# Two batches' kv in one call: k and v of batch 5 loaded with batch 4 in a fused linear-attention and MLP kernel

## The chip, the cores and the metric

One NeuronCore of one Trainium2 chip runs the kernel. The metric is the device time of one execution in microseconds. Three runs of the kernel before took 288.9, 288.96 and 289.06 us, so the median is 288.96 us.

## The reference

There are eight batches, eight heads, 576 positions and a head dimension of 64. The first half is linear attention with a norm for each head, the second a two-layer MLP with a layer norm and a residual:

```python
kv = np.einsum('bhsd,bhse->bhde', k, v)
out = np.einsum('bhsd,bhde->bhse', q, kv)
rms = np.sqrt(np.mean(out * out, axis=-1, keepdims=True) + 1e-06)
x = (out / rms * g_norm)          # heads side by side: [8, 576, 512]
xn = (x - mu) / np.sqrt(var + 1e-06) * g_ln
result = x + np.maximum(xn @ w_ch1, 0.0) @ w_ch2    # 512 -> 2048 -> 512
```

So batch b's kv needs all of k and v of that batch, and every row of its output needs that kv.

## The kernel before

**Tiles.** Each batch has 576 positions: four tiles of 128 positions and a remainder of 64. The remainders of two batches are put together into one remainder tile of 128 (`rem_tile`, L364; tile 3 joins batches 2 and 3), and the four remainder tiles make a ninth block called "rem", which the MLP takes last.

**A batch's way to the MLP.** `load` (L92) brings one tensor of a batch into one of two buffers, `k_in`, `v_in` or `q_in` with index b % 2, in two DMAs issued from POOL that also cast f32 to bf16: 320 KB and 256 KB as stored. `kv_of` (L240) makes the kv of one or more batches with 40 matmuls of 64 columns each into one PSUM tile (L247), and copies it to `kv_pack[b % 4]` on ACT (L252, L253). `turn_q_dma` (L202) copies q on DVE into another order (L204) and has SP issue a DMA transpose (L206) that gives `qt`. A tile's work is planned by `plan_tile` (L374) in four steps: the matmuls of q with kv (`o`, L274) with the squares and their sums; the scaling to x and its normed copy `xc`; the variance; and a transpose of `xc` into `xT_blk`, which for the later batches is a DMA transpose issued from SP (L355).

**The MLP.** `mm1` (L406) multiplies the four tiles' `xT_blk` with the first weight (L416) and ACT applies the relu (L419); `mm2` (L455) multiplies with the second weight (L432), DVE adds the residual in `finish` (L437), and the result is stored by DMA from SP (L452, L453).

**The order of the work.** A hand-written agenda sets it. `at(slot, fn)` (L474) files a function under a slot, and `tick` (L477), which mm1 and mm2 call once for every four full-width matmuls, emits what is due before the next matmuls. Each batch takes 32 slots: mm1 of batch b from slot 32b on, and mm2 from 32b + 16 on. All engines execute in the order of emission, and each waits for semaphores of the others. So a function filed under slot 85 puts its TensorE work in the middle of mm2 of batch 2, and its DMAs and copies behind whatever was emitted before on their own engines.

**The gate ahead of a load.** `load_batches` (L96) first copies one element of something to `gate` on POOL (L98), for example the last element of a batch's turned q. POOL can't issue the loads behind it until that has been written. Loads of one call go out in the order of the list.

The part that the change touches is the list of loads (L641 to L647), the list of kv calls with their remainder tiles (L650 to L653), and the list of q turns with their batches' tiles (L658 to L663).

Of the kernel before, what the change touches and what calls it, by code (L numbers as in the profile page):

```python
# [14 lines left out]
def kernel(  # L15
# [76 lines left out]
    def load(dst, t, b, h0=0, h1=H):  # L92
        nc.gpsimd.dma_start(dst[:64, h0:h1], lo(t, b, h0, h1))
        nc.gpsimd.dma_start(dst[64:, h0:h1, :J], up(t, b, h0, h1))

    def load_batches(what, *after):  # L96
        for element in after:
            nc.gpsimd.tensor_copy(gate, element)  # L98
        tensors = {"k": (k_in, k), "v": (v_in, v), "q": (q_in, q)}
        for name, b in what:  # L100
            dst, src = tensors[name]
            load(dst[b % NB], src, b)
# [99 lines left out]
    def turn_q_dma(b):  # L202
        q_p = kv_in.tile([128, JJ, H, D], bf16, tag="qp", bufs=2)
        nc.vector.tensor_copy(q_p.rearrange("p j h d -> p h j d"), q_in[b % NB])  # L204
        q_t = qt_pool.tile([128, JJ, HP, 128], bf16, tag="qt", name="qt")
        nc.sync.dma_start_transpose(  # L206
            q_t.rearrange("p j hp t -> p (j hp) t"), q_p.rearrange("p j h d -> p (j h d)"))
        qts[b] = q_t
# [31 lines left out]
    def kv_of(*bs):  # L240
        kv_ps = ps_m.tile([128, len(bs), HP, D], f32, tag="misc", name="kv_ps")
        for i, b in enumerate(bs):
            for hp in range(HP):
                for j in range(JJ):
                    for hh in range(2):
                        h = 2 * hp + hh
                        nc.tensor.matmul(  # L247
                            kv_ps[hh * D:hh * D + D, i, hp, :], lhsT=k_in[b % NB][:, h, j, :],
                            rhs=v_in[b % NB][:, h, j, :], start=(j == 0), stop=(j == JJ - 1))
        for i, b in enumerate(bs):  # L250
            kvp = held[b] = kv_pack[b % 4]
            nc.scalar.copy(kvp[:D, :, :D], kv_ps[:D, i])  # L252
            nc.scalar.copy(kvp[D:, :, D:], kv_ps[D:, i])  # L253
# [104 lines left out]
    def main_tile(b, j, pool=None, tag="ops"):  # L358
        q_t, kvp = qts[b], held[b]
        if b not in blks:  # L360
            blks[b] = new_block("main", 3)
        return Tile([(slice(0, 128), lambda hp: q_t[:, j, hp, :], kvp)], blks[b], j, pool, tag)

    def rem_tile(b):  # L364
        mms = []
        for half, bb in enumerate((b - 1, b)):
            qt, kp = qts.pop(bb), held.pop(bb)
            mms.append((slice(half * 64, (half + 1) * 64),
                        lambda hp, qt=qt: qt[:, J, hp, :64], kp))
        if "rem" not in blks:  # L370
            blks["rem"] = new_block("rem", 1)
        return Tile(mms, blks["rem"], b // 2)

    def plan_tile(s, make, turn_at, on_pe, x_at=None):  # L374
        box = []

        def first():
            t = make()
            box.append(t)
            t.o()  # L380
            t.sq()
            t.red()

        def second():
            t = box[0]
            t.y()
            t.x()
            t.xc()

        def third():  # L390
            box[0].var()

        def fourth():
            box[0].turn(on_pe)

        at(s, first)
        at(x_at or s + 2, second)
        at((x_at or s + 2) + 4, third)
        at(turn_at, fourth)
# [22 lines left out]
    def rstd_of(b):  # L422
        rstd = work.tile([128, 4], f32, tag="rstd", bufs=3, name="rstd")
        nc.scalar.activation(rstd, blks[b][1][:, 2, :], func=AF.Sqrt, scale=1.0 / Dm, bias=eps_sb)  # L424
        nc.vector.reciprocal(rstd, rstd)  # L425
        rstds[b] = rstd
# [47 lines left out]
    def at(slot, fn):  # L474
        agenda.setdefault(int(slot), []).append((slot, fn))
# [162 lines left out]
    def turned_q(b):  # L638
        return qts[b][:1, J, HP - 1, 127:]

    at(47, lambda: load_batches((("k", 3), ("v", 3), ("q", 3)), turned_q(2)))  # L641
    at(68, lambda: load_batches((("k", 4), ("v", 4), ("q", 4)),
                                turned_q(3), blks[2][2][:1, nK - 1, 511:]))
    at(100, lambda: load_batches((("k", 5), ("v", 5), ("q", 5)), turned_q(4)))
    at(132, lambda: load_batches((("q", 6), ("k", 6), ("v", 6), ("k", 7), ("v", 7)),
                                 turned_q(5)))
    at(164, lambda: load_batches((("q", 7),), turned_q(6)))  # L647


    at(115, lambda: kv_of(5))  # L650
    for s, bs, rem, x_at, tn in ((56, (3,), 1, 64, 69), (85, (4,), 3, 88, 94),
                                 (152, (6, 7), 5, 154, 160)):
        at(s, lambda bs=bs: kv_of(*bs))  # L653
        plan_tile(s + .1, lambda rem=rem: rem_tile(rem), tn, False, x_at)
    plan_tile(210, lambda: rem_tile(7), 216, False)


    for b, at_q, at_o, step in ((3, 56.05, 67, 4.3), (4, 86, 97, 4.75),  # L658
                                *((b, 32 * b - 43.3, 32 * b - 32, 5) for b in range(5, B))):
        at(at_q, lambda b=b: turn_q_dma(b))  # L660
        for j in range(J):
            o = at_o + step * j
            plan_tile(o, lambda b=b, j=j: main_tile(b, j), o + 6, False)  # L663
        at(32 * b + 14, lambda b=b: rstd_of(b))
# [59 lines left out]
```

## Time and profile before

| what | value |
|---|---|
| median of three runs | 288.96 us |
| the profiled execution's own time | 288.75 us |
| its span, first to last instruction | 286.7 us |
| TensorE matmul busy | 277.8 us (97%) |
| VectorE, ScalarE, GpSimd busy | 150.0, 152.9, 43.1 us |
| granted TensorE clock | 1.000 |
| bytes read from HBM, written | 36.71 MB, 9.44 MB |
| one load of 320 KB, issue to landing (median) | 8.7 to 10.3 us |
| one DMA transpose of a tile (median) | 3.2 us |
| one DMA transpose of a batch's q (median) | 5.1 us |

The span is what the profile's times refer to; 2.05 us of the profiled execution's own time lie outside it. Times in a timeline are from the start of the span. A row names the start, the duration, the engine, the line, the operation, what it writes and reads, and how many instructions are merged in it; in brackets stands how long the engine had been idle before, and what ended that. A few matmul records are missing from the trace, so a row that should have 20 can show 19. PE is the matmul part of TensorE, PEld its weight loads. SP issues most stores and all the DMA transposes of this kernel, POOL issues the loads; their DMA rows show the issue, and the landing is shown apart in the DMA view.

In the trace, mm2 of batch 2 begins near 95.7 us, mm1 of batch 3 at 110.62, mm2 of batch 3 at 125.33 and mm1 of batch 4 at 140.23.

### The profile page before, as it was taken

To read this page: it belongs to the slowest core of one execution; us is meant where nothing else is said; L and a number is where in the kernel's file an instruction comes from. 1 tells how busy PE (TensorE), PEld (TensorE's weight loads), DVE (VectorE), ACT (ScalarE), POOL (GpSimd) and SP (SyncE) were. 2 spreads that over 40 slices of the span, in tenths; PEclk is the share of its full clock that TensorE was granted. 3 is DMA by queue.
4 is the path that set the end of the run, shared out by engine and by line. 5 is a ranking of instruction groups with operands and counts; after the bars stand their busy time and mean duration, and the time that the engine had idled before them with its cause. 6 is when DMAs were issued, how large, how long until landed. Compare 5 with 4: busy or idle time off the path is not lost.

```text
span 286.7 us, 5727 instructions
## 1 busy us (share of the span) xinstructions
PE 277.8 (97%) x2269; PEld 158.0 (55%) x2295; DVE 150.0 (52%) x331; ACT 152.9 (53%) x333; POOL 43.1 (15%) x73
## 2 busy tenths in 40 slices
PE   7889999999999999999999999999999999999995
PEld 3579755995579654454444544444444444444444
DVE  5774119937997883774376475763679200220022
ACT  3477844995468643971387338911893066016500
POOL 8522510041036005000710020000000000000000
PEclk9999999999999999999999999999999999999999
DMA  7999999969997979986999995047203410230033
GB/s 215 198 209 202 201 191 197 214 111 188 144 180 124 185 141 172 214 101 127 159 215 190 120 160 135 18 82 158 56 18 72 95 37 0 48 81 19 0 73 76
DMA packets 67419, 36.76 MB, mean 128 GB/s; under 512 B 35517, under 2 KB 62525, under 8 KB 67393
## 3 DMA queue, kind: packets, MB, share of 16 engines
q0 software_dynamic: 28720, 18.29, 44.2%
q1 hardware_dynamic: 38160, 17.39, 30.4%
q10 hardware_dynamic: 512, 0.72, 0.8%
q8 instruction: 18, 0.29, 0.5%
q14 instruction: 9, 0.07, 0.1%
HBM read 36.71 MB, written 9.44 MB: 161 GB/s over the span
## 4 chain that ended last, share of the span: by engine, by line
PE 91%; DMA 2%; DVE 2%; ACT 2%; issue 1%; DVEq 0%; POOLq 0%
PE p L432 43%; PE p L416 42%; PE o_ps L274 3%; DMA v_in<-in_v_dram 2%; PE kv_ps L247 2%; ACT m L419 1%; DVE x_blk L292 0%; DVE xc L552 0%; ACT xT_blk L353 0%; PE tp L351 0%; ACT rms L311 0%; PE odd L226 0%; DVE ss L518 0%; PE tp L559 0%; DVE ss L301 0%
## 5 line engine op out<-in xcount | busy, mean ns | idle before, releaser
L416 PE MATMUL p<-xT_blk,w_sb 128*128 128x128 bf16 (+2 forms) x1015 | 131.2, 285 | 0.9
L432 PE MATMUL p<-w_sb,m 128*128 128x512 bf16 (+2 forms) x592 | 126.2, 368 | 1.2 <-issue 0.5
L419 ACT ACTIVATE m<-p 128x512 bf16<-128x512 f32 x144 | 85.2, 596 | 46.7 <-PE p L416 44.3
L416 PEld LDWEIGHTS <-w_sb 128*128 128x128 bf16 x1024 | 78.6, 98 | 44.5 <-issue 1.1
L432 PEld LDWEIGHTS <-m 128*128 128x128 bf16 x608 | 57.3, 98 | 62.9
L437 DVE SCALAR_TENSOR_TENSOR o_sb<-p,rstd,x_blk 128x512 f32<-128x512 f32 (+2 forms) x38 | 27.2, 721 | 47.7 <-PE p L432 42.1
L280 ACT ACTIVATE sq<-o_ps 128x512 f32<-128x512 f32 x35 | 20.9, 596 | 26.7 <-PE o_ps L274 26.5
L343 ACT ACTIVATE dev<-x_blk,st_blk 128x512 f32<-128x512 f32 x36 | 25.7, 714 | 13.1 <-DVE st_blk L329 13.1
L301 DVE TENSOR_REDUCE ss<-sq 128x8 f32<-128x512 f32 x35 | 23.7, 678 | 17.0 <-ACT sq L280 17.0
L335 DVE SCALAR_TENSOR_TENSOR xc<-x_blk,st_blk,g_ln_sb 128x512 bf16<-128x512 f32 x34 | 25.6, 752 | 1.2
L306 DVE TENSOR_TENSOR y<-o_ps,inv 128x512 f32<-128x512 f32 x33 | 22.8, 692 | 3.1
L325 DVE SCALAR_TENSOR_TENSOR x_blk<-y,g_norm_sb 128x512 f32<-128x512 f32 x33 | 22.8, 692 | 1.1
L318 DVE RECIPROCAL inv<-rms 128x8 f32<-128x8 f32 x36 | 7.3, 202 | 23.3 <-ACT rms L311 23.3
L425 DVE RECIPROCAL rstd<-rstd 128x4 f32<-128x4 f32 x9 | 1.6, 175 | 29.9 <-ACT rstd L424 29.8
L311 ACT ACTIVATE rms<-ss,eps_sb 128x8 f32<-128x8 f32 x36 | 10.6, 295 | 11.5 <-DVE ss L301 11.3
L274 PEld LDWEIGHTS <-qt 128*128 128x128 bf16 (+1 forms) x156 | 10.3, 100 | 6.0 <-issue 0.4
L274 PE MATMUL o_ps<-kv_pack,qt 128*128 128x128 bf16 (+1 forms) x156 | 13.6, 220 | 0.0
L98 POOL COPY gate<-qt 1x1 bf16<-1x1 bf16 x5 | 0.9, 177 | 82.4 <-DMA qt<-q_p 82.4
L199 PE MATMUL p<-fill_sb 128*128 128x512 bf16 x26 | 7.8, 452 | 1.3 <-DVE eps_sb L138 1.2
L252 ACT CAST kv_pack<-kv_ps 64x256 bf16<-64x256 f32 x7 | 2.6, 366 | 10.7 <-PE kv_ps L247 10.7
L343 ACT ACTIVATION_READ_ACCUMULATOR dev<-x_blk,st_blk 128x1 f32 x36 | 6.8, 190 | 0.0
L247 PEld LDWEIGHTS <-k_in 128*64 128x64 bf16 x280 | 4.9, 112 | 2.4 <-issue 2.3
(82 smaller groups left out, 112.6 us busy)
## 6 DMA issues: line engine op xcount, KB each, us to landing
out_dram<-o_sb SPq DMA_DIRECT2D x66, 128.0 KB, 2.6
w_sb<-in_moe_w_ch_dram POOLq DMA_DIRECT2D x8, 512.0 KB, 15.2
q_in<-in_q_dram POOLq DMA_DIRECT2D x7, 320.0 KB, 9.7
k_in<-in_k_dram POOLq DMA_DIRECT2D x7, 320.0 KB, 8.7
v_in<-in_v_dram POOLq DMA_DIRECT2D x7, 320.0 KB, 10.3
q_in<-in_q_dram POOLq DMA_DIRECT2D x8, 256.0 KB, 10.5
k_in<-in_k_dram POOLq DMA_DIRECT2D x7, 256.0 KB, 9.3
v_in<-in_v_dram POOLq DMA_DIRECT2D x7, 256.0 KB, 12.3
```

The lines of the kernel that those rows point to most:

```text
L247: nc.tensor.matmul(kv_ps[hh * D:hh * D + D, i, hp, :], lhsT=k_in[b % NB][:, h, j, :], rhs=v_in[b % NB][:, h, j, :], start=(j == 0), stop=( ...
L274: nc.tensor.matmul(flat[rows, hp * 128:(hp + 1) * 128], lhsT=lhsT_of(hp), rhs=kvp[:, hp, :], start=True, stop=True)
L280: nc.scalar.activation(self.sq_t, self.o_ps, func=AF.Square)
L301: nc.vector.tensor_reduce(self.ss, self.sq_t, axis=AX.X, op=ALU.add)
L306: nc.vector.tensor_mul(self.y_t, self.o_ps, self.inv().to_broadcast([128, H, D]))
L325: nc.vector.scalar_tensor_tensor(x_blk[:, ts].rearrange("p (h d) -> p h d", h=H), in0=self.y_t, scalar=1.0, in1=g_norm_sb.to_broadcast([12 ...
L335: nc.vector.scalar_tensor_tensor(self.xc_t, in0=x_blk[:, self.ts], scalar=st[:, 1, self.ts:self.ts + 1], in1=g_ln_sb, op0=ALU.add, op1=ALU ...
L343: nc.scalar.activation(dev, x_blk[:, ts], func=AF.Square, bias=st[:, 1, ts:ts + 1], accum_out=st[:, 2, ts:ts + 1])
L416: nc.tensor.matmul(p1[:, i, :], lhsT=w1_sb[:, kk, de * 128:(de + 1) * 128], rhs=blk[2][:, kk, sl], start=(kk == 0), stop=(kk == nK - 1))
L419: nc.scalar.activation(m1[:, de0:de0 + per, sl], p1, func=AF.Relu)
L432: nc.tensor.matmul(p2[:, c0:c1], lhsT=m1s[b][:, de, ts * 128:(ts + 1) * 128], rhs=w2_sb[:, de, c0:c1], start=(de == 0), stop=(de == nDe - 1))
L437: nc.vector.scalar_tensor_tensor(o_sb[:, c0:c1], in0=p2[:, c0:c1], scalar=rstds[b][:, ts:ts + 1], in1=blks[b][0][:, ts, c0:c1], op0=ALU.mu ...
```

## The change

The change moves entries of the agenda and nothing else: the same instructions are executed, in another order.

- k and v of batch 5 are loaded in the call at slot 68, behind k, v and q of batch 4, instead of at slot 100.
- q of batch 5 is loaded at slot 101, with k and v of batch 6 behind it, which were in the call at slot 132. The call at slot 132 has three tensors left.
- The kv of batches 4 and 5 is made in one call at slot 93. Before, it was batch 4's at slot 85 and batch 5's at slot 115. Remainder tile 3 stays behind the call, at 93.1 instead of 85.1; its second step is at slot 95 and its transpose at 101, instead of 88 and 94.
- q of batch 4 is turned at slot 92 instead of 86, and batch 4's four tiles start at slot 101 with a step of 4.3, instead of 97 and 4.75.

```diff
-    at(68, lambda: load_batches((("k", 4), ("v", 4), ("q", 4)),
+    at(68, lambda: load_batches((("k", 4), ("v", 4), ("q", 4), ("k", 5), ("v", 5)),
                                 turned_q(3), blks[2][2][:1, nK - 1, 511:]))
-    at(100, lambda: load_batches((("k", 5), ("v", 5), ("q", 5)), turned_q(4)))
-    at(132, lambda: load_batches((("q", 6), ("k", 6), ("v", 6), ("k", 7), ("v", 7)),
+    at(101, lambda: load_batches((("q", 5), ("k", 6), ("v", 6)), turned_q(4)))
+    at(132, lambda: load_batches((("q", 6), ("k", 7), ("v", 7)),
                                  turned_q(5)))
...
-    at(115, lambda: kv_of(5))
-    for s, bs, rem, x_at, tn in ((56, (3,), 1, 64, 69), (85, (4,), 3, 88, 94),
+    for s, bs, rem, x_at, tn in ((56, (3,), 1, 64, 69), (93, (4, 5), 3, 95, 101),
                                  (152, (6, 7), 5, 154, 160)):
...
-    for b, at_q, at_o, step in ((3, 56.05, 67, 4.3), (4, 86, 97, 4.75),
+    for b, at_q, at_o, step in ((3, 56.05, 67, 4.3), (4, 92, 101, 4.3),
                                 *((b, 32 * b - 43.3, 32 * b - 32, 5) for b in range(5, B))):
```

On TensorE this takes the interruption for kv at slot 115 away and makes the one of slot 85 twice as long, at slot 93. On SP the turn of batch 4's q moves behind the stores of the second and third tile of batch 2, and the transpose of remainder tile 3 behind it and behind the stores of the last tile. On DVE the copy of batch 4's q follows the finish of batch 2's first three tiles, where it followed that of the first. On POOL four loads move ahead of one gate, and four more ahead of another.

## Prediction

> **What bounds the kernel now.** I read the page's first table first: TensorE is busy 97% of the span, and its waits view, asked for PE alone, is short:
>
> ```profile
> PE 277.8 (97%) x2269; PEld 158.0 (55%) x2295; DVE 150.0 (52%) x331; ACT 152.9 (53%) x333; POOL 43.1 (15%) x73
> ```
>
> ```profile
> PE even L226 <- DMA v_in<-in_v_dram: 1.4, 1, 1.4
> PE p L199 <- DVE eps_sb L138: 1.2, 1, 1.2
> PE p L432 <- issue: 0.5, 3, 0.2
> PE tp L559 <- DVE xc L552: 0.4, 1, 0.4
> ```
>
> All waits but the 0.5 us of "issue" lie in the first 18 us. From slot 80 on no transfer holds TensorE, so the time is the sum of its work, and the only gain to be had near the change is what an interruption of the matmul stream costs beyond its work. Second, the timeline of PE through that stage (start, us, what, number of instructions):
>
> ```profile
> 94.85 1.04 PE L416 MATMUL p<-xT_blk,w_sb 128*128 128x256 bf16 x8
> 95.94 4.26 PE L432 MATMUL p<-w_sb,m 128*128 128x512 bf16 x19
> 100.14 0.82 PE L247 MATMUL kv_ps<-v_in,k_in 128*64 128x64 bf16 x40
> ...
> 110.62 1.03 PE L416 MATMUL p<-xT_blk,w_sb 128*128 128x512 bf16 x4
> ...
> 125.33 2.75 PE L432 MATMUL p<-w_sb,m 128*128 128x512 bf16 x12
> 128.01 0.82 PE L247 MATMUL kv_ps<-v_in,k_in 128*64 128x64 bf16 x40
> 129.00 11.17 PE L432 MATMUL p<-w_sb,m 128*128 128x512 bf16 x50 [0.16 <-issue]
> 140.00 0.39 PE L274 MATMUL o_ps<-kv_pack,qt 128*128 128x128 bf16 x4
> ...
> 154.71 7.07 PE L432 MATMUL p<-w_sb,m 128*128 128x512 bf16 x31
> 161.71 1.46 PE L247 MATMUL kv_ps<-v_in,k_in 128*64 128x64 bf16 x80
> 163.00 0.39 PE L274 MATMUL o_ps<-kv_pack,qt 128*64 128x128 bf16 x8
> ```
>
> kv of 4 starts at 100.14, kv of 5 at 128.01, the pair (6, 7) at 161.71. A slot is four full-width matmuls; 20 of them take 4.31 us between 115.39 and 119.70 elsewhere in this view, so one is 0.2155 us and a slot 0.862 us.
>
> Third, POOL's timeline, which has the loads' issue times:
>
> ```profile
> 88.22 0.71 POOL L93 DMA_DIRECT2D k_in<-in_k_dram  x1 [1.14 <-PE o_ps L274]
> ...
> 91.61 0.75 POOL L94 DMA_DIRECT2D q_in<-in_q_dram  x1
> ...
> 137.61 0.68 POOL L93 DMA_DIRECT2D q_in<-in_q_dram  x1 [0.34 <-DVE o_sb L437]
> ...
> 145.65 0.68 POOL L94 DMA_DIRECT2D v_in<-in_v_dram  x1 [1.12 <-DMA q_in<-in_q_dram]
> ```
>
> and the DMA view of the windows that hold the two last issues (KB, us from issue to landing):
>
> ```profile
> q_in<-in_q_dram POOLq DMA_DIRECT2D x1, 256.0 KB, 10.6
> ...
> v_in<-in_v_dram POOLq DMA_DIRECT2D x1, 256.0 KB, 14.0
> ```
>
> So the six transfers for batch 4 run from 88.22 to 91.61 + 10.6 = 102.2. The five-tensor load at slot 132, ten transfers, runs from 137.61 to 145.65 + 14.0 = 159.65: 22.0 us. Its kv is at 161.71, 2 us later; that one just fits.
>
> [...] the load queue moves 0.39 MB in 119 to 121, where it is alone, and 0.26 MB in 94 to 96, where a DMA transpose from SP moves 0.10 MB beside it. [...] The trace shows only that a 1.4 us wait left the granted clock at 1.00; it has no longer wait.
>
> **The change part by part.**
>
> Step 1, merging two kv calls. Work is unchanged: 80 matmuls. Kv of 5 alone: from 125.33 to 140.00 are 14.67 us for 64 matmuls of 0.2155 (13.79), so it costs 0.88. Kv of 4 with remainder tile 3: the eight half-width matmuls from 94.85 end near 95.72, next stage at 110.62, 14.90 - 13.79 = 1.11. The pair with its remainder tile, 154.71 to 170.24 (start of the next o group): 15.53 - 13.79 = 1.74. Gain: 0.88 + 1.11 - 1.74 = **0.25 us**.
>
> Step 2, k and v of 5 behind q of 4. The gate ahead (q of 3 turned, last transpose of batch 2 landed) is unchanged, so the first issue stays at 88.22. Four issues of 0.67 us follow 91.61, the last two held until k of 4 has landed, as the ninth and tenth wait at 143.84 and 145.65 for the first two of their set; k of 4 lands by 94.5, so all are issued by about 95, long before DMA gets to them. They are 2 x (320 + 256) KB = 1.18 MB behind the 102.2 at which q of 4 lands. Alone at 0.196 MB/us (0.39 in 2 us) they need 6.0 us: 108.2, the earliest. SP's traffic is in the way: the end of one DMA transpose, the stores of batch 2's first two tiles (0.26 MB each) and the last transpose of batch 3, issued at 103.62 now. A transpose is 0.13 MB at 0.05 MB/us: 2.5 us in which the loads run at 0.133 and lose 0.8 us; a store pair costs them about 0.7 us (144.5 to 147: 0.35 MB of loads beside 0.26 MB of stores). All four: 108.2 + 3.0 = 111.2, the latest. The ten-transfer set gives 88.22 + 22.0 = 110.2. I take **110.5**, between that set and the full sum, because SP's queue is busy all through 101.5 to 110 (1.26 MB).
>
> Step 3, when TensorE wants them. With kv of 4 gone from slot 85, slot 93 comes 32 matmuls later: 100.14 + 32 x 0.2155 = 107.04. The 40 matmuls of batch 4 take 0.65 us (161.71 to 163.00 is 1.29 for 80). In the built order the first weight load of batch 5, and the matmul behind it, wait for its four transfers: at **107.7**. New wait: 110.5 - 107.7 = **2.8 us**, from 0.5 (108.2) to 3.5 (111.2). Queued behind it on PE are remainder tile 3, the last of mm2 of batch 2 and all else; nothing can pass. ACT's kv copies and DVE's finish wait with it, at no further cost.
>
> Step 4, batch 4's q turned at slot 92 instead of 86. DVE's copy (0.82 us) now follows the finishes of the first three tiles of batch 2, so SP gets the transpose near 108.3 (before: 105.02), behind two more stores. It took 4.9 us before; beside loads a transpose took 7.8, so it lands at 113 to 116. Its tiles start at slot 101: mm1 of batch 3 starts at 110.62 + (1.74 - 1.11) + 2.8 = 114.05, slot 101 at 118.4. Covered by 2 us at least, cost nothing; without the stall of step 3 slot 101 is at 115.6, and up to 0.5 us would show.
>
> Step 5, the last transpose of batch 3 (issue 103.62) now shares DMA with k and v of 5: up to 7.8 us, 111.4. It is wanted at 114.05: hidden by the stall; without it 0.2 us.
>
> Step 6, tiles of batch 4 at 101 to 113.9 instead of 97 to 111.25. Same instructions; ACT has one square fewer within mm1 of batch 3, where TensorE ran without a gap anyway. The last transpose is queued on SP behind that of q of 5, as before (135.10, landed 137.6 for a need at 140.00), and all of it shifts alike. Nothing.
>
> Step 7, later loads. POOL's gate opens after batch 4's turned q, about 114 to 116 instead of 109.9, but q of 5 is first now, not third: landed some 7 us later, near 122, for a turn at slot 116.7 (128 or later). The set at slot 132 is two tensors shorter, so it lands earlier. Nothing.
>
> **Sum.** -0.25 + 2.8 = +2.55 us, all on TensorE. The profiled execution took 288.75 us, span 286.7 and 2.05 around it; it becomes 291.3, span 289.25. The median of the runs shown is 288.96, 0.2 above the profiled one: **291.5**.
>
> **Rivals.** (B) Batch 5's v is in time. It needs the four transfers in 5.5 us after 102.2, 0.21 MB/us, against 0.196 alone: only if the loads of batch 4 finish earlier than in this trace. Then only step 1 is left: 288.96 - 0.25 = **288.7**, not slower. It decides below a landing of 107.95. For it: the wait is at the end of the merged call, and the same pair at slot 152 has no wait. Against: there the load has 24.1 us, here 19.5.
> (C) Only a short wait: SP's stores and transposes slip behind the loads, landing 108.5 to 109.4, wait 0.8 to 1.7, time about **290.0**.
> (D) [...] wait 3.7, [...]: +5.15, **294.1**. For it: queue 1 is fully loaded. Against: the full sum of step 2 ends at 3.5[...].
>
> **Numbers.** A measurement of this kernel can tell about 0.2%, 0.6 us, from no change. Forecast (wait of 1.8 to 3.6 us, 290.5 to 292.4): 0.62. C: 0.13. B, with waits below 0.8: 0.15. D: 0.10. The range from 289.4 to 293.3 leaves out B and half of D. Slower: forecast, C, D: 0.84, allowing 0.01 of C to stay within. Same: 0.14. Faster by over 0.2%: 0.02, since the whole of step 1 is 0.25 us.
>
> **What would show it.** A PE wait on a DMA of v_in (or k_in) at L247 of 2 to 3.5 us near 107.7; 80 kv matmuls in two groups with the gap between them; v of 5's second half landing near 110.5; mm1 of batch 3 starting near 114; no wait at L274 for qt near slot 101; granted clock still 1.00. I am wrong if v of 5 lands before 108.5, or if another PE wait appears, or if the clock falls.

## The result, and the profile after

| | before | after |
|---|---|---|
| median of the runs | 288.93 us (4 runs) | 296.75 us (4 runs) |
| ratio | | 1.0272, 95% interval 1.0234 to 1.031 |
| profiled execution, its span | 288.75, 286.7 us | 297.45, 295.3 us |
| granted TensorE clock | 1.000 | 0.988 |

The change costs 7.8 us, three times the forecast of 2.55. The direction was right; the time lies outside the range of 289.4 to 293.3. The ratios leave out one execution, of the kernel with twelve dummy matmuls, that is over 1.5% above the fastest of its kernel (298.99 us).

The first table of the page after, and its row of granted clock (40 slices of the span, in tenths):

```profile
PE 280.8 (95%) x2269; PEld 159.3 (54%) x2295; DVE 149.7 (51%) x331; ACT 153.0 (52%) x333; POOL 43.1 (15%) x73
...
PEclk9999999999999995999999999999999999999999
```

The number of matmul records is the same, yet TensorE is busy 3 us longer, and one slice of the clock shows 5: some matmuls ran at half speed. PE's waits after (total, times, longest):

```profile
PE kv_ps L247 <- DMA v_in<-in_v_dram: 4.6, 1, 4.6
...
PE p L432 <- DVE o_sb L437: 0.7, 1, 0.7
```

Two waits are new: one on v at the merged kv call, where the prediction put it but longer, and one on VectorE's finish, which it did not have. Where they lie is in the timeline of PE after:

```profile
96.72 11.17 PE L432 MATMUL p<-w_sb,m 128*128 128x512 bf16 x50
107.82 0.82 PE L247 MATMUL kv_ps<-v_in,k_in 128*64 128x64 bf16 x40
113.27 1.28 PE L247 MATMUL kv_ps<-v_in,k_in 128*64 128x64 bf16 x40 [4.63 <-DMA v_in<-in_v_dram]
...
115.31 4.08 PE L432 MATMUL p<-w_sb,m 128*128 128x512 bf16 x11 [0.33 <-issue]
119.22 4.48 PE L416 MATMUL p<-xT_blk,w_sb 128*128 128x512 bf16 x20
...
134.56 0.39 PE L274 MATMUL o_ps<-kv_pack,qt 128*128 128x128 bf16 x4
134.79 6.21 PE L432 MATMUL p<-w_sb,m 128*128 128x512 bf16 x27
141.65 7.07 PE L432 MATMUL p<-w_sb,m 128*128 128x512 bf16 x31 [0.66 <-DVE o_sb L437]
148.55 0.39 PE L274 MATMUL o_ps<-kv_pack,qt 128*128 128x128 bf16 x4
```

Batch 4's 40 matmuls run at 107.82 and need 0.65 us. Batch 5's start at 113.27, 4.80 us after that. (The 4.63 in brackets counts from the end that the profile gives the last matmul, 0.17 later.) From there to mm1 of batch 3 at 119.22 are 5.95 us, for work that takes 3.69 at full clock (0.65 of kv, 0.45 of remainder tile 3, twelve matmuls of 0.2155). The table by stretch after gives the reason (us, then busy time and count of PE, PEld, DVE, ACT and POOL, the granted clock, DMA share, GB/s):

```profile
108.50:113.20 4.70, 0.14 (x10) 0.03 (x2) 0.05 (x1) 0.00 (x0) 0.00 (x0) 0.83 1.43 217
113.20:118.40 5.20, 4.80 (x56) 2.78 (x58) 1.19 (x3) 2.37 (x6) 1.78 (x4) 0.50 0.62 112
```

The clock was 0.50 while TensorE caught up. In the clock's records of the trace the half lasts from 111.58 to 118.41, 6.83 us, of which the first 1.7 cost nothing since TensorE was waiting.

**The bill.** The q matmuls with which mm1 of batch 4 opens begin 8.55 us later than before (148.55 against 140.00):

| term | us |
|---|---|
| opening: mm2 of batch 2 starts at 96.72 instead of 95.94, with the same instructions ahead | 0.78 |
| TensorE idle before batch 5's kv | 4.80 |
| half clock after it, 5.95 - 3.69 | 2.26 |
| wait for VectorE's finish at 141.65 | 0.66 |
| one interruption for kv fewer, as forecast | -0.25 |
| small gaps, not assigned | 0.30 |
| sum | 8.55 |

The opening is not of the change: executions of the kernel before differ by as much (spans of 286.6 to 287.8 us), and in the traces of the other kernels that have the same work up to there, mm2 of batch 2 starts anywhere from 95.50 to 96.73. Without it 7.77 are left, against 7.82 between the medians.

### The profile page after: what moved, and what is told of

Read it like the earlier page. It is cut to its first block, busy times and chain, and to the rows that moved or that the text cites. A ratio compares the mean times of both kernels' runs of the same rounds, so it can differ in the third digit from the quotient of the medians.

```text
span 295.3 us, 5727 instructions
## 1 busy us (share of the span) xinstructions
PE 280.8 (95%) x2269; PEld 159.3 (54%) x2295; DVE 149.7 (51%) x331; ACT 153.0 (52%) x333; POOL 43.1 (15%) x73
## 4 chain that ended last, share of the span: by engine, by line
PE 80%; DMA 10%; DVE 4%; ACT 2%; issue 2%; POOL 0%; DVEq 0%; POOLq 0%
PE p L416 38%; PE p L432 36%; DMA v_in<-in_v_dram 9%; PE o_ps L274 2%; DMA k_in<-in_k_dram 2%; PE kv_ps L247 2%; ACT m L419 1%; DVE x_blk L292 0%; DVE x_blk L325 0%; DVE y L306 0%; DVE xc L552 0%; ACT rms L311 0%; DVE ss L301 0%; DVE o_sb L437 0%; ACT xT_blk L353 0%
## 5 line engine op out<-in xcount | busy, mean ns | idle before, releaser
L432 PE MATMUL p<-w_sb,m 128*128 128x512 bf16 (+2 forms) x591 | 128.0, 371 | 1.9 <-DVE o_sb L437 0.7
L247 PE MATMUL kv_ps<-v_in,k_in 128*64 128x64 bf16 x280 | 6.0, 203 | 4.6 <-DMA v_in<-in_v_dram 4.6
L199 PE MATMUL p<-fill_sb 128*128 128x512 bf16 x26 | 8.5, 483 | 1.3 <-DVE eps_sb L138 1.2
L247 PEld LDWEIGHTS <-k_in 128*64 128x64 bf16 x280 | 5.4, 119 | 6.5 <-issue 6.4
```

What stands on the lines that cost most here:

```text
L247: nc.tensor.matmul(kv_ps[hh * D:hh * D + D, i, hp, :], lhsT=k_in[b % NB][:, h, j, :], rhs=v_in[b % NB][:, h, j, :], start=(j == 0), stop=( ...
L432: nc.tensor.matmul(p2[:, c0:c1], lhsT=m1s[b][:, de, ts * 128:(ts + 1) * 128], rhs=w2_sb[:, de, c0:c1], start=(de == 0), stop=(de == nDe - 1))
```

## The experiments

### How much of the loss is the clock, and what lowers it

Twenty, then twelve dummy matmuls stand between the two batches' kv, so that TensorE is idle for less of the same wait. They are work that the kernel doesn't need.

```diff
         for i, b in enumerate(bs):
+            if b == 5:
+                dummy = fill(20, ps1.tile([128, 512], f32, tag="p1", name="dummy"))
+                del dummy
```

> The changed kernel with 20 dummy matmuls of 128x512 (4.3 us) put between the kv of batch 4 and that of batch 5, into a PSUM tile that nobody reads; the output is the same. Theory: the wait for batch 5's v lets the clock fall to half, and 5.95 us of work then run where 3.7 would do, 2.3 us lost. With TensorE kept busy the load lands at the same time, the clock stays at 1.00, and the span falls from 295.3 to about 293.0 (time 294.5 to 295.0). Rival (the clock falls for another reason than the idle time): the half clock stays, and the time with it, 296.7. Rival (the clock costs nothing, all is the wait): 296.7 with the clock at 1.00.

> The changed kernel with 12 dummy matmuls (2.6 us) between the kv of batch 4 and of batch 5, where 20 kept the clock up; the output is the same. About 2.8 us of the wait are left idle, as much as was forecast for the changed kernel. Theory: [...] it stays at 1.00 in most runs, and the time is that with 20 dummies, 294.5 to 295.5. Rival (already a shorter gap lowers it): half clock for 3.4 us or more in the trace, 296.5 and up.

With twenty: 295.28 us, ratio 1.022 (1.0197 to 1.0242), clock 0.998 to 1.000. Its timeline of PE:

```profile
113.56 0.82 PE L250 MATMUL kv_ps<-v_in,k_in 128*64 128x64 bf16 x40 [1.46 <-DMA v_in<-in_v_dram]
114.54 2.76 PE L435 MATMUL p<-w_sb,m 128*128 128x512 bf16 x12
117.14 4.48 PE L419 MATMUL p<-xT_blk,w_sb 128*128 128x512 bf16 x20
```

Batch 5's kv starts as late as in the changed kernel, but the same stretch up to mm1 of batch 3 takes 3.58 us instead of 5.95. So the 2.3 us are the clock's, and it fell because TensorE stood idle. The medians differ by 1.5 us only, and the time is 0.3 above the range that was expected: v landed 0.3 us later in this trace, a wait of 0.2 us for the turned q of batch 5 appeared, and the rest is not assigned. With twelve, 295.4 us (1.0206, 1.0168 to 1.0243): 1.9 us of waiting at L250, and clocks of 1.000, 0.998 and 0.994 in the three executions compared. A clock of 0.994 is what one half-speed stretch of 3.41 us makes of a span of 293, so some 2 us of idle time may be at the edge; only the first of the three has a trace.

### What makes v of batch 5 late

First, without the stores of the first three tiles of batch 2 (these rows of the output are left out); second, without the later of the two gates ahead of the loads, so that they start earlier.

```diff
+        if b == 2 and ts < 3:
+            return
```

```diff
-                                turned_q(3), blks[2][2][:1, nK - 1, 511:]))
+                                turned_q(3)))
```

> The changed kernel without the stores of batch 2's first three tiles (0.79 MB on SP's queue), so those rows of the output are left out. Theory: SP's stores share the DMA engines with the loads of k and v of batch 5; a pair was put at 0.7 us, so batch 5's v lands 1.5 to 2 us earlier after the first issue of its set (22 to 22.7 us instead of 24.1) and the wait at L247 falls from 4.6 us to about 3. The clock may then stay full: 290.5 to 292.5 where it does, 294 to 295 where it doesn't. Rival (the loads' own volume and the transposes set the landing): landing 24 us after the first issue, time 296 to 297.

> The changed kernel with only one gate ahead of the load at slot 68: it waits for batch 3's turned q, no longer for the last transpose of batch 2 (landed 87.6, so the first issue was at 89.0). Theory: the landing of batch 5's v is set by when the set starts and by what it shares the DMA engines with; the start moves up to about 86, the landing by 2 to 3 us to 110.5 or 111, the wait at L247 shrinks from 4.6 to about 2 us, and with it the stretch of half clock, to one window or none: 292 to 294.5, unless the loads delay that last transpose of batch 2, which would show as a wait at L416 near 88. Rival (the start doesn't matter, since the DMA engines are the bound from 82 on): landing at 113, 296 to 297.

Without the stores: 293.91 us, ratio 1.0176 (1.0147 to 1.0204). v of 5 lands 22.05 us after the first issue, where it takes 24.12 in the changed kernel. The last of its transfers is issued at 94.88 here and at 95.75 there, 6.47 and 6.73 us after the first; how long it took is in the DMA views, first of the changed kernel, then of this one:

```profile
v_in<-in_v_dram POOLq DMA_DIRECT2D x1, 256.0 KB, 17.4
...
v_in<-in_v_dram POOLq DMA_DIRECT2D x1, 256.0 KB, 15.6
```

These are single traces. In the six other traces with the same loads, gates and stores the landing is 23.27 to 25.27 us after the first issue, so leaving the stores out is worth some 1 to 3 us. Up to 18 us after the first issue both had moved the same (2.50 and 2.52 of the 2.95 MB of loads), so the 2 us are lost at the end, where the stores are, and with them the hole that is described below. The wait, and the table by stretch of this kernel:

```profile
PE kv_ps L247 <- DMA v_in<-in_v_dram: 2.5, 1, 2.5
```

```profile
107.90:110.50 2.60, 0.15 (x10) 0.04 (x4) 0.06 (x1) 0.00 (x0) 0.00 (x0) 1.00 1.23 162
...
111.30:114.60 3.30, 2.97 (x21) 1.36 (x17) 0.69 (x1) 2.32 (x6) 1.31 (x3) 0.50 0.36 72
```

TensorE was idle for 2.7 us, from 107.88 to 110.59, and the clock was halved for 3.41 us from 111.27 on, when TensorE was already at work again. The four executions had clocks of 0.988 to 0.994. So a wait of the size that was forecast, 2.8 us, can halve the clock too.

Without the later gate: 296.04 us, 1.0247 (1.0225 to 1.0268), a miss. The first issue is at 85.63, some 3 us earlier than in the changed kernel, and v of 5 lands at 112.13, 26.5 us after it:

```profile
PE kv_ps L247 <- DMA v_in<-in_v_dram: 4.3, 1, 4.3
```

Issuing 3 us earlier brought 1 us of landing, of which 0.7 is only the shorter opening of this execution (kv of 4 is at 107.11, not 107.82), and 0.3 us of wait. So the gate does not set the landing; that what the DMA engines have to carry by slot 93 sets it is the likely reading, which the run without stores supports.

### A stretch in which the DMA engines moved next to nothing

In the changed kernel the load of v contains a hole. The DMA view after, from 109.1 to 110 us (packets and MB; then for each queue its packets, MB, and the time that they took):

```profile
DMA packets 80, 0.03 MB, mean 34 GB/s; under 512 B 45, under 2 KB 80, under 8 KB 80
...
q1 hardware_dynamic: 43, 0.01, 131.7%
q0 software_dynamic: 37, 0.02, 87.8%
```

Of the 56 packets issued from 109.1 to 109.3, 32 ended together at 110.02 to 110.12, where others take up to some 0.1 us: loads and SP's packets hung for 0.85 us, and 34 GB/s were left. A packet of 16 KB on q8, the queue of instructions, a fetch, had started at 108.26 and ended at 109.21. The same pair, 0.6 to 0.9 us apart, is near slot 93 in the traces of nine kernels here; without the stores the fetch is there (107.88) and the hole isn't. To see whether the hole belongs to the fetch, the fetch was moved by making the program longer at its start:

```diff
-    fill(18)
+    p0 = fill(16)
+    for _ in range(64):
+        nc.tensor.matmul(p0[:32, :16], lhsT=fill_sb[:, :32], rhs=fill_sb[:, :16], start=True, stop=True)
+    del p0
```

> The changed kernel with 124 more TensorE instructions at its very start (two full-width dummy matmuls fewer, 64 matmuls of 16 columns with their weight loads more), so that each later 16 KB instruction fetch of TensorE[...], falls some 124 instructions earlier in the work: the one at 108.3 should come near 103 to 104. Theory (the 0.85 us in which all loads and SP packets hang follow the fetch): the hang moves with it, to about 0.9 us after the fetch, near 104 to 105, and no hang is at 109 to 110. v of 5 then lands at about the same time, 24 us after the first issue, since the hang still lies within the loads. Rival (the hang belongs to the mix of stores and loads at that point, or to TensorE's idle time): it stays near 109 to 110 wherever the fetch is. The time is no test: the opening is some 2 us different.

298.03 us in one execution, a time that is no test. The fetch came at 98.69, 9.6 us earlier and so further than expected. At 109 to 110 the loads and stores went on:

```profile
109.00:110.00 1.00, 0.68 (x40) 0.56 (x36) 0.58 (x1) 0.00 (x0) 0.00 (x0) 1.00 1.31 185
```

So the hole is not of the stores and loads at that point, and the rival falls. Nor is there one behind the moved fetch, as the theory had it: at 98.7 SP moved next to nothing (five packets in the 0.75 us after it), and the loads ran on at 0.18 MB/us. But another fetch of this kernel has moved to 43.80, where loads and a transpose run together, and there is a hole of 1.3 us behind it that no other trace has.

The fourteen traces have 196 fetches from 40 us on. Groups of 20 or more packets that each took over 0.5 us and ended together are found in 25 places, each of them behind a fetch that began at most 1.1 us before the first of these packets, and each with a DMA transpose in flight. Sixteen groups are of loads and SP's packets together. The other nine are of SP's packets alone, with no load in flight; the changed kernel has one behind a fetch at 171.89, beside a turn of q. Its DMA view from 172.5 to 173.6:

```profile
DMA packets 29, 0.01 MB, mean 7 GB/s; under 512 B 29, under 2 KB 29, under 8 KB 29
```

Other fetches that met loads and a transpose left no such group, among them the one at 107.88 in the kernel without stores, and groups of up to 18 packets occur without a fetch as well. So in these traces the hole came with a fetch that met a DMA transpose, with or without loads, though not each time; what stops the packets no run shows. Nor do the runs show what it costs: v of 5 landed 23.64 us after the first issue here, 0.5 less than in the changed kernel, but one of the traces that do have the hole shows 23.27.

### Whether the rest of the change is free

Four kernels take the wait for v away or leave it out. The merged call later, at slot 100:

```diff
-    for s, bs, rem, x_at, tn in ((56, (3,), 1, 64, 69), (93, (4, 5), 3, 95, 101),
+    for s, bs, rem, x_at, tn in ((56, (3,), 1, 64, 69), (100, (4, 5), 3, 102, 107),
```

> The changed kernel with the common kv of 4 and 5 at slot 100 instead of 93, remainder tile 3 behind it. Theory: everything but 0.4 to 0.7 us comes from the wait at this place; seven slots later, near 113.5, the last half of batch 5's v has landed (113.1 in the changed kernel's trace), so no wait over 0.3 us at L247, clock 1.00, and 288.9 - 0.25 + 0.66 (finish of batch 3's first tile late) = 289.3. Rival (the moved tiles, the moved turn of q and the loads cost the time): still 293 or more.

292.89 us, 1.0137 (1.012 to 1.0154), clock 0.998 to 1.000. v of 5 lands at 112.25 for a call at 114.73, and no wait is left at L247. But:

```profile
PE p L416 <- DMA xT_blk<-xc: 1.5, 1, 1.5
PE p L432 <- DVE o_sb L437: 1.2, 1, 1.2
...
PE p L416 <- ACT m L419: 0.8, 1, 0.8
```

The first is the last transpose of batch 3, which took 8.2 us beside the loads (2.5 in the kernel before) and which the wait for v had hidden. Against 289.3 expected, this is a miss.

The merge undone in the changed kernel, with batch 5's kv back at slot 115; and the kernel before with only the new places of batch 4's kv, remainder tile 3, q turn and tiles:

```diff
-    for s, bs, rem, x_at, tn in ((56, (3,), 1, 64, 69), (93, (4, 5), 3, 95, 101),
+    at(115, lambda: kv_of(5))
+    for s, bs, rem, x_at, tn in ((56, (3,), 1, 64, 69), (93, (4,), 3, 95, 101),
```

```diff
-    for s, bs, rem, x_at, tn in ((56, (3,), 1, 64, 69), (85, (4,), 3, 88, 94),
+    for s, bs, rem, x_at, tn in ((56, (3,), 1, 64, 69), (93, (4,), 3, 95, 101),
...
-    for b, at_q, at_o, step in ((3, 56.05, 67, 4.3), (4, 86, 97, 4.75),
+    for b, at_q, at_o, step in ((3, 56.05, 67, 4.3), (4, 92, 101, 4.3),
```

> The changed kernel with batch 5's kv taken out of the common call and put back at slot 115, all else as changed: loads, q turn and tiles. Theory: batch 5's v has until slot 115, so no wait, clock 1.00; what stays is the late finish of batch 3's first tile, 0.66 us in the trace: 288.9 + 0.66 = 289.6. Rival (loads and moved tiles cost): 293 or more. If the late finish came from the stall, 288.9.

> The kernel before with only the places changed: kv of 4 with remainder tile 3 at slot 93, batch 4's q turned at 92, its tiles from 101 with a step of 4.3; loads and kv of 5 as before. Theory: the chain of a tile on VectorE and ScalarE takes 3.7 us and up, the tiles now come every 3.9 us and end 2.65 slots later, so the finish of batch 3's first tile is queued behind the last tile's chain and PE waits for its buffer about 0.66 us near slot 120: 288.9 + 0.66 = 289.6. If that wait came from the stall alone: 288.9.

They give 290.51 us (1.0062, 1.0041 to 1.0083) and 290.68 us (1.0058, 1.0043 to 1.0073), 1.6 and 1.8 us more than the kernel before, which took 288.87 beside them, and some 1 us more than was expected of either. The second one's new wait of TensorE in this stage:

```profile
PE p L432 <- DVE o_sb L437: 0.9, 1, 0.9
```

The wait for the finish is there with no early load and no merged call, so it comes with the tiles' places and not from the stall. In the kernel with the merge undone it is 0.9 us as well, with 0.4 for the last transpose of batch 3. The second kernel has another new wait, one stage later, of 0.7 us at the pair (6, 7): batch 7 is loaded there behind the turn of batch 5's q, which comes later (gate open at 140.56, before at 137.10), and its v landed at 164.13. So of the 1.8 us 0.9 are the finish and 0.7 this load.

The last of the four files the tiles with a step of 4.4 slots instead of 4.3, in the kernel with the merge undone, so that the last tile's work on VectorE comes behind the first finish:

```diff
-    for b, at_q, at_o, step in ((3, 56.05, 67, 4.3), (4, 92, 101, 4.3),
+    for b, at_q, at_o, step in ((3, 56.05, 67, 4.3), (4, 92, 101, 4.4),
```

> The split kernel (kv of 5 back at slot 115) with the tiles' step 4.4 instead of 4.3. The last tile's scaling is then filed at 116.2, behind the finish of batch 3's first tile, and no longer at 115.9, ahead of it. Theory: the wait of 0.85 us for that finish is only this order on VectorE, so it goes: 290.5 - 0.85 = 289.65. Rival (VectorE is simply short of time there): 290.5, with a wait of 0.5 us or more for a finish.

290.48 us, 1.0057 (1.0038 to 1.0076): nothing won, where 289.65 was expected. The wait for the finish is gone, and 0.8 us stand at 142.80, where mm1 of batch 4 needs its last tile:

```profile
142.80 4.48 PE L416 MATMUL p<-xT_blk,w_sb 128*128 128x512 bf16 x19 [0.77 <-PE o_ps L274]
```

The line names PE's own q matmuls, but these had begun at 141.65; that tile's transpose was issued at 140.21, behind the turn of batch 5's q and two stores, and landed at 142.71. A delay of about the same size comes out one stage later.

### Whether another order of the loads saves it

k and v of 5 ahead of q of 4, with q's turn and its tiles later to suit; then that order with one gate only, an earlier turn of batch 4's q and a later one of batch 5's (second diff, against the changed kernel too). The first also loads q of 5 at slot 104 instead of 101:

```diff
-    at(68, lambda: load_batches((("k", 4), ("v", 4), ("q", 4), ("k", 5), ("v", 5)),
+    at(68, lambda: load_batches((("k", 4), ("v", 4), ("k", 5), ("v", 5), ("q", 4)),
...
-    for b, at_q, at_o, step in ((3, 56.05, 67, 4.3), (4, 92, 101, 4.3),
+    for b, at_q, at_o, step in ((3, 56.05, 67, 4.3), (4, 97, 104, 4.4),
```

```diff
-                                turned_q(3), blks[2][2][:1, nK - 1, 511:]))
+                                turned_q(3)))
...
-    for b, at_q, at_o, step in ((3, 56.05, 67, 4.3), (4, 92, 101, 4.3),
+    for b, at_q, at_o, step in ((3, 56.05, 67, 4.3), (4, 94.5, 101, 4.4),
...
-        at(at_q, lambda b=b: turn_q_dma(b))
+        at(120.6 if b == 5 else at_q, lambda b=b: turn_q_dma(b))
```

> The changed kernel with k and v of batch 5 loaded ahead of batch 4's q, which is then turned at slot 97, and batch 4's tiles from slot 104 with a step of 4.4. Theory: the fourth transfer of batch 5 is now the eighth of the set; in the traces so far the eighth landed 17.9 to 19.1 us after the first issue, near 106.5, and it is wanted 19.5 after it, so there is no wait at L247 over 0.3 us and the clock stays at 1.00. The price is a late q: it lands near 112, its turn near 118, for a want near 118. 288.9 - 0.25 + 0 to 1.5 = 288.7 to 290.2. Rival (not the order of the loads but the common call itself costs): a wait of 4 us stays and 295 or more.

> The changed kernel mended as the runs suggest: one gate ahead of the set at slot 68; k and v of batch 5 ahead of batch 4's q in it; q of 4 turned at slot 94.5; its tiles with a step of 4.4; q of 5 turned at slot 120.6, behind batch 4's last transpose on SP. Theory: v of 5 lands near 104 to 105, wanted at 107.7, no wait at L247; q of 4 lands near 110 and its turn near 116, where slot 101 is: 0 to 1 us of wait at L274; no finish wait. 288.9 - 0.25 + 0 to 1.5: 288.7 to 290.2, clock 1.00. It can't be measurably faster than before, since the merge gives 0.25 us at most. Rival (the common call or its place costs something else): 292 or more without a wait over 1 us.

304.41 us (1.0521, 1.0489 to 1.0552) and 292.28 us (1.0112, 1.0087 to 1.0137), both misses. v of 5 is there in time in both, landed at 106.76 and 106.14. What is late is q:

```profile
PE p L416 <- DMA xT_blk<-xc: 4.6, 1, 4.6
PE o_ps L274 <- DMA qt<-q_p: 3.8, 1, 3.8
```

These are the first kernel's waits, and each is followed by 6.83 us of half clock in its trace. The second kernel waits for qt in two places, 2.2 and 1.4 us, and keeps its clock. None of these is as fast as the kernel before.

### What one interruption for kv costs

The kernel before merges batches 6 and 7 at slot 152. Here they are split, with batch 7 alone at slot 166; nothing waits for a load in either.

```diff
+    at(166, lambda: kv_of(7))
...
-                                 (152, (6, 7), 5, 154, 160)):
+                                 (152, (6,), 5, 154, 160)):
```

> The kernel before with the one merged kv call that it has, batches 6 and 7 at slot 152, split: batch 6 with remainder tile 5 at slot 152, batch 7 alone at slot 166. k and v of 7 land at 159.7 and so are there for both. It measures the first step of the prediction the other way round. Theory: an interruption of its own costs 0.25 us beyond its 40 matmuls, so the two stages around slots 144 to 176 take 0.25 us longer together, with no wait at L247, and the time is 288.9 + 0.25 = 289.2 (0.1% slower, at the limit of what can be told). Rival (the merge is worth much more, since each interruption also makes ScalarE's and VectorE's work late): over 0.6 us.

288.95 us beside 288.79 (12 and 14 runs, ratio 1.0001, 0.999 to 1.0013). The trace is finer than the times. The two ends of the stage with the kv calls split:

```profile
154.86 7.07 PE L432 MATMUL p<-w_sb,m 128*128 128x512 bf16 x32
...
185.32 13.98 PE L432 MATMUL p<-w_sb,m 128*128 128x512 bf16 x64
```

That is 30.46 us. In the kernel before it lasts from 154.71 to 184.95, 30.24, and in the eleven other traces with this merged pair and no wait there it is 30.23 or 30.24. The end in the kernel before:

```profile
184.95 13.98 PE L432 MATMUL p<-w_sb,m 128*128 128x512 bf16 x63
```

An interruption of its own costs 0.22 us, so a merge of two gives about that here.

## Why the prediction was wrong, point by point

- **Step 1, the merge: right.** 0.25 us forecast, 0.22 measured by splitting the other pair.
- **Step 2, the landing of v: too early by 1.84 us, and the first term that failed.** The loads took 24.12 us from first issue to landing, not 22.28 (110.5 less 88.22). Without stores they took 22.05, so the value taken left almost no room for the stores. The step had its full sum at 23.0 and chose 110.5 "between that set and the full sum", which took 0.7 back. It counted the stores of two tiles; the third tile's were issued at 107.85, inside the load, another 0.7 by its own price. These two make 1.4 of the 1.84. The other 0.4 lie within the spread from trace to trace (23.27 to 25.27), and whether the hole in DMA has part in them stays open; in the trace of before the fetch of this stage came at 102.0, when the loads were just done, and left none.
- **Step 3, the wait: right in place, mis-sized by step 2.** Kv of 4 came at 107.82, and batch 5 was wanted at 108.47, 0.77 later than forecast; but the first issue was 0.80 later too, so the two cancel. 2.8 + 1.84 is the 4.63 us that the timeline has in brackets.
- **The clock, the forecast's "granted clock still 1.00": wrong.** Rival D was a halved clock, at a chance of 0.10 and with a wait of 3.7 us; for it the prediction has queue 1 fully loaded, where in the trace of before that queue's packets took 77.0% of the engines' time from 101.5 to 110. That the forecast's own wait of 2.8 us would leave the clock at 1.00 was the author's estimate: the longest wait in the trace of before is 1.4 us. Without the stores 2.7 us of idle time halved the clock for 3.41 us, so at 2.8 us a half clock could have been due already. In the changed kernel it lasted 6.83 us and cost 2.26 us.

  The traces also show what counts in place of the gap's length. In all fourteen, each stretch between two changes of the clock is a whole number of 3.413 us (31, 2 and 52 in the changed kernel, 83 in the kernel before), so the changes lie on a grid with that step. The table by stretch for single steps of these grids, up to a change or where one could have come: the changed kernel, the one without stores, two of the one without the later gate, twelve dummies, and the last kernel of the section on the order of loads:

```profile
108.17:111.58 3.41, 0.47 (x30) 0.36 (x24) 0.38 (x1) 0.00 (x0) 0.00 (x0) 1.00 1.54 164
...
107.86:111.27 3.41, 0.87 (x55) 0.79 (x50) 0.10 (x1) 0.00 (x0) 0.00 (x0) 1.00 1.26 195
...
106.31:109.72 3.41, 1.62 (x45) 0.91 (x42) 1.49 (x2) 0.00 (x0) 0.00 (x0) 1.00 1.40 164
109.73:113.14 3.41, 0.87 (x48) 0.90 (x48) 0.00 (x0) 0.01 (x1) 0.00 (x0) 1.00 1.07 250
...
109.73:113.15 3.42, 1.47 (x19) 0.62 (x19) 0.00 (x0) 0.00 (x0) 0.00 (x0) 1.00 1.19 261
...
116.02:119.43 3.41, 1.45 (x10) 0.83 (x11) 0.54 (x2) 1.34 (x4) 1.10 (x3) 1.00 0.98 196
```

  The first busy time is PE's. Behind the steps with 0.47, 0.87 and 0.87 us of it the clock fell; behind those with 1.62, 1.47 and 1.45 it stayed up. So in these six a gap cost by how much of one step it emptied. The 4.3 us without the later gate straddle a border and brought one stretch of half clock of 3.41 us; in the changed kernel the wait went on into the next step, to 113.27, and a second such stretch followed. A wait that the profile gives as 2.2 us, in the last kernel, brought none, where the one it gives as 2.5, without the stores, brought one. No run moved a gap against the grid on purpose.
- **Step 4, batch 4's q turn: right that it is covered.** The first of the tiles starts at 123.53 with no wait for qt.
- **Step 5, batch 3's last transpose: right that the stall hides it, wrong in its size without the stall.** It landed at 111.87 (forecast 111.4). Uncovered it was 0.4 us with kv of 4 alone at slot 93 and 1.5 with the merged call moved behind it, not 0.2.
- **Step 6, the tiles' places: wrong, 0.66 us instead of nothing.** The step looked at ScalarE and at mm1 of batch 3. With the last tile at slot 113.9 its q matmuls fall in mm2 (134.56 above), and its work on VectorE stands ahead of the first finish. VectorE's timeline after:

```profile
140.18 0.75 DVE L335 SCALAR_TENSOR_TENSOR xc<-x_blk,st_blk,g_ln_sb 128x512 bf16<-128x512 f32 x1
140.85 0.75 DVE L437 SCALAR_TENSOR_TENSOR o_sb<-p,rstd,x_blk 128x512 f32<-128x512 f32 x1
```

  The finish frees the PSUM buffer for which TensorE waits until 141.65. The tiles' places without the loads and the merge bring such a wait of 0.9 us.
- **Step 7, later loads: right.** q of 5 landed at 122.66 for a turn at 141.51.

In sum: 2.55 forecast, plus 1.84 (step 2), 2.26 (clock), 0.66 (step 6) and 0.3 not assigned, is 7.6 of the 7.8 measured; the bill has 0.17 more since it counts the idle time as 4.80. The 0.3 stay open, as does what a fetch of instructions has to do with the hole in DMA.

## What to carry to other kernels

A load that is moved ahead is priced by all the traffic it will meet until it lands, stores of the later landing time included, and where that sum and a milder guess differ, the sum is kept. A wait on TensorE had a second price behind it here, the half clock. A wait that the profile gives as 2.5 us was enough for it and one of 2.2 wasn't. How much work was left in one step of 3.41 us, 0.87 us or less where the clock fell and 1.45 or more where it stayed up, told more than the length of the gap. A tile that is moved across a stage's border takes its vector work along, which then stands ahead of the next stage's first finish, so every engine's queue at that border is looked through.

## What was not expected of the hardware

- TensorE's clock halved after an idle stretch of 2.7 us, the lowering coming 0.7 us after work had begun again, and stayed halved for 3.41 or 6.83 us. In each trace all its changes lie on a grid of 3.413 us.
- A fetch of instructions, a packet of 16 KB (18 of them on q8 in the page before), went with a hole in DMA: behind the one of 0.95 us at 108.26 loads and SP's transfers hung for some 0.85 us. Such groups of loads and SP's packets together are found sixteen times in the fourteen traces, and nine times more with SP's packets alone; in each case a DMA transpose was in flight.
